# Down projection of the second chunk as seven f16 products, with its operand sums spread over ten pairs of units, and a fourth gate buffer for the other chunks

## The chip, the cores and the metric

The kernel runs on one core of a Trainium2 chip. A core has a matrix engine (TensorE, PE in the profile), a vector engine (VectorE, DVE), a scalar engine (ScalarE, ACT), a general engine (GpSimd, POOL) and a sync engine (SyncE, SP). Each runs its own queue of instructions in order; they wait for each other by semaphores. SP, ACT and POOL can issue transfers (DMAs) between main memory and the on-chip memories SBUF and PSUM. TensorE writes to PSUM, which has eight banks of 128 x 512 float32.

The metric is the device time of one execution in microseconds (us); lower is better. A time is given as the median of several executions.

## The reference

```
x  : 2048 x 448          wq : 448 x 4096      wo : 4096 x 448
k_cache, v_cache : 8 heads x 2048 x 256
w_gate, w_up : 448 x 1792                     w_down : 1792 x 448

xn = layernorm(x)
q  = xn @ wq                      16 heads of 256, two to each k/v head
k, v = the last 512 positions of the caches
o  = softmax(q k^T / 16) v
s  = o @ wo
g  = silu((gelu(xn @ w_gate) * (xn @ w_up)) @ w_down)
out = x + s * g
```

The change is in `g`: in the product with `w_down`, for 512 of the 2048 rows.

## The kernel before

The 2048 rows are 16 tiles of 128, and four chunks of 512 rows (`QC`, `NQC`). The kernel first computes `g` for all rows (the feed-forward stage), stores it to main memory (`g2d`, called g_all in the profile), then does the attention head by head, and at the end of each chunk the output projection with the rows' `g` (`burst`).

**Feed-forward.** The 1792 columns of w_gate and w_up are 14 blocks of 128 (`NF`). A unit is one block for one chunk: both products x w_gate and x w_up, into two banks. There are 56 units, numbered n, and the loop takes them in pairs (n, n+1); four are done ahead of it. The loop alternates between two sets of four banks, `cur` and `nxt`. The units of chunk 0 are 0 to 13, of chunk 1 14 to 27, of chunk 2 28 to 41, of chunk 3 42 to 55. After the matmuls of a pair (`gu_group`), ScalarE applies gelu to the gate bank (into `gl`, three buffers) and VectorE multiplies it with the up bank into `actT` (`gu_evac`, L522 and L523). `actT` holds two chunks, by chunk number modulo 2, in bf16. In the loop VectorE also does the layer norm of the later tiles (`ln_a`, `ln_b`, up to n = 28), ScalarE casts w_o to f16 (`cast_wt`, 16 casts), and VectorE forms sums of the cast parts (`sum_wt`, 16 sums). `CASTS` and `SUMS` are lists with the n from which each may be done; one or two are taken for each pair.

**Down projection.** `down(c, pairs)` multiplies the 512 rows of chunk c with w_down: for each of the four tiles 14 matmuls of 448 columns into a bank, then tanh on ScalarE (L533), then (tanh + 1) times the bank on VectorE into `g2w` (L534), then a store from SP into `g2d` (L537). `g2w` has three buffers (`NXR`), taken by the tile number modulo 3. `DOWN_AT` places it: chunk 0 after the pair n = 18, chunk 1 after n = 28. Chunks 2 and 3 follow within the first two steps of the attention loop (m = 0 and 1).

**Output projection.** `burst` already computes o @ wo by seven products instead of eight: both operands are cut in two halves in each direction, certain sums and differences of the quarters are formed beforehand by VectorE (`sums`, `sum_wt`), and seven products of quarters in f16, added up with signs, give the result.

**Queues and order.** The program order of each engine is the order in which the Python code calls `K.op`. `Plan` records what each operation reads and writes and makes it wait for the operations it depends on; `K.reuse` does that for memory that held something else. SP holds, in this order: the first loads, the transposes of the layer norm, the stores of the first two down projections, from n = 32 all loads of w_q, V and K (K is transposed on the way), then the transposes of the attention's probabilities (`dma_t` in `s_mm`) and the stores of the last two down projections. POOL holds the loads of w_o (`load_wt` at n = 14 and 30), then the loads of `g2` and x (`load_g2`, `xr`).

Of the kernel before, what the change touches and what calls it, by code (L numbers as in the profile page):

```python
# [5 lines left out]
ACT = mybir.ActivationFunctionType  # L6
ALU = mybir.AluOpType
BF16 = mybir.dt.bfloat16
F32 = mybir.dt.float32
F16 = mybir.dt.float16  # L10

LN_EPS = 1e-5
P = 128
# [155 lines left out]
def bass_recurrent_scan__sliding_block_cached__geglu_ffn__prompt_kernel(  # L169
# [12 lines left out]
    _, S, D = A_x.shape  # L182
    Hkv, Sk, Dh = A_k_cache.shape[1], A_k_cache.shape[2], A_k_cache.shape[3]
# [3 lines left out]
    F = B_w_gate.shape[1]  # L187
    NT = S // P
    QC = 512
    NQC = S // QC  # L190
    NF = F // P
    NJ = W // P
# [10 lines left out]
    NG = Hq // HG  # L203
    QS = 8
    Q0 = 4
    HC = QC // 2
    N2 = D // 2
    WS = 64.0

    es = ExitStack()  # L210
    with es:
        K = Plan(nc, es)
        base = [(nc.sbuf_base + 31) // 32 * 32]

        def place(name, shape, dt, at=None):
            size = {BF16: 2, F16: 2, F32: 4}[dt]
            for n in shape[1:]:
                size *= n
            size = (size + 31) // 32 * 32
            if at is None:  # L220
                at = base[0]
                base[0] += size
            assert at + size <= nc.sbuf_usable_end, (name, at + size, nc.sbuf_usable_end)
            return nc.alloc_sbuf_tensor_at(name, list(shape), dt, offset=at), at, at + size

        def sbuf_bufs(at, size, n):
            return [K.buf(at + i * size, size) for i in range(n)]
# [5 lines left out]
        ident, a_ident, _ = place("ident", [P, P], BF16)  # L233
        b_ident = K.buf(a_ident, 256)
        nhalf, a, _ = place("nhalf", [P, 1], F32)
        b_nhalf = K.buf(a, 4)
        epst, a, _ = place("epst", [P, 1], F32)
        b_epst = K.buf(a, 4)
        stats, a, _ = place("stats", [P, NT, 6], F32)
        b_stats = sbuf_bufs(a, 24, NT)  # L240
        mv, a, _ = place("mv", [P, NT, 2], F32)
        b_mv = sbuf_bufs(a, 8, NT)
        ve, a, _ = place("ve", [P, NT], F32)
        b_ve = sbuf_bufs(a, 4, NT)
        rstd, a, _ = place("rstd", [P, NT], F32)
        b_rstd = sbuf_bufs(a, 4, NT)
        NRS = 8
        rsum, a, _ = place("rsum", [P, NRS], F32)
        b_rsum = sbuf_bufs(a, 4, NRS)
        rden, a, _ = place("rden", [P, NRS], F32)  # L250
        b_rden = sbuf_bufs(a, 4, NRS)

        xnT, a, _ = place("xnT", [P, NK + 1, S], BF16)
        b_xnT = [[K.buf(), K.buf()] for t in range(NT)]
        NG2 = 2
        g2, a, _ = place("g2", [P, NG2, D], BF16)
        b_g2 = sbuf_bufs(a, D * 2, NG2)
        g2d = nc.dram_tensor("g2_all", [NT, P, D], BF16)
        b_g2d = [K.buf() for t in range(NT)]
        kT, a, _ = place("kT", [P, Hkv, 2, W], BF16)  # L260
        b_kT = sbuf_bufs(a, 2 * W * 2, Hkv)
        va, a, _ = place("va", [P, Hkv, NJ, Dh], BF16)
        b_va = [K.buf() for g in range(Hkv)]
        wq, a, _ = place("wq", [P, NK, HD], BF16)
        wqr, a, _ = place("wqr", [P, Hq, P], BF16)
        b_wql = [[K.buf() for i in range(3)] for g in range(NG)]
        NXR = 3
        xr, a, _ = place("xr", [P, NXR, D], BF16)
        b_xr = [[K.buf(a + (i * D + lo) * 2, (hi - lo) * 2) for lo, hi in ((0, CUT), (CUT, D))] for i in range(NXR)]
        g2w, _, _ = place("g2w", [P, NXR, D], BF16, at=a)  # L270
        b_g2w = sbuf_bufs(a, D * 2, NXR)
        tmp, a, _ = place("tmp", [P, 2, QC], F32)
        b_tmp = sbuf_bufs(a, QC * 4, 2)

        rw = base[0]
        NB = 4
        wt, _, rw_end = place("wt", [P, 7, Hq, N2], F16)
# [21 lines left out]
        b_wd = K.buf(a, at - a)  # L299
        actT, a, at = place("actT", [P, 2, NF, QC], BF16, at=at)  # L300
        b_actT = [sbuf_bufs(a + i * NF * QC * 2, QC * 2, NF) for i in range(2)]
        NGL = 3
        gl, a, at = place("gl", [P, NGL, QC], BF16, at=at)
        b_gl = sbuf_bufs(a, QC * 2, NGL)


        NPT, NPN, NP32 = 3, 3, 3
        pT, a, at = place("pT", [P, NPT, 2, 2, NJ, P], BF16, at=rf)
# [32 lines left out]
        def dma(q, o, i, reads=(), writes=()):  # L341
            K.op(q, lambda e, o=o, i=i: e.dma_start(o, i), reads, writes, dma=True)
# [4 lines left out]
        def act(o, i, func, reads, writes, scale=1.0):  # L347
            K.op("act", lambda e, o=o, i=i: e.activation(o, i, func, scale=scale), reads, writes)  # L348

        def add(eng, o, x, y, reads, writes, op=ALU.add):  # L350
            K.op(eng, lambda e: e.tensor_tensor(o, x, y, op), reads, writes)

        def mms(lst, reads, writes, after=()):
            def fn(e):
                ins = None
                for (o, l, r, st, sp) in lst:
                    ins = e.matmul(o, lhsT=l, rhs=r, start=st, stop=sp, skip_group_check=True)  # L357
                return ins
            return K.op("pe", fn, reads, writes, after=after)
# [159 lines left out]
        def gu_evac(n, b):  # L519
            c, f = divmod(n, NF)  # L520
            s = n % NGL
            act(gl[:, s, :], bank[b], ACT.Gelu_apprx_tanh, (b_ps[b],), (b_gl[s],))  # L522
            K.op("dve", lambda e: e.tensor_tensor(actT[:, c % 2, f, :], bank[b + 1], gl[:, s, :], ALU.mult),  # L523
                 (b_ps[b + 1], b_gl[s]), (b_actT[c % 2][f],))

        def down(c, pairs):
            for t4 in range(4):
                t = c * 4 + t4
                b = bk(pairs, t4)
                mms([(bank[b][:, 0:D], actT[:, c % 2, f, t4 * P:(t4 + 1) * P], wd[:, f, :], f == 0, f == NF - 1)  # L530
                     for f in range(NF)], [b_wd] + b_actT[c % 2], (b_ps[b],))
                s = t % 2
                act(tmp[:, s, 0:D], bank[b][:, 0:D], ACT.Tanh, (b_ps[b],), (b_tmp[s],), scale=0.5)  # L533
                K.op("dve", lambda e, t=t, b=b, s=s: e.scalar_tensor_tensor(  # L534
                    out=g2w[:, t % NXR, :], in0=tmp[:, s, 0:D], scalar=1.0, in1=bank[b][:, 0:D],
                    op0=ALU.add, op1=ALU.mult), (b_tmp[s], b_ps[b]), (b_g2w[t % NXR],))
                dma("sp", g2d[t], g2w[:, t % NXR, :], (b_g2w[t % NXR],), (b_g2d[t],))  # L537

        def ln_first(t):
            ln_stats(t)  # L540
# [58 lines left out]
        def load_k(g):  # L599
            dma_t(kT[:, g, :, :], A_k_cache[0, g, Sk - W:Sk, :], (), (b_kT[g],))  # L600

        def load_v(g):
            dma("sp", va[:, g, :, :],
                A_v_cache[0, g, Sk - W:Sk, :].rearrange("(j p) d -> p j d", p=P), (), (b_va[g],))

        def load_wq(g):
            lo, hi = g * HG * Dh, (g + 1) * HG * Dh
            dma("sp", wq[:, :, lo:hi], A_wq[0:K3, lo:hi].rearrange("(k p) f -> p k f", p=P), (), (b_wql[g][0],))
            for e in range(2):
                dma("sp", wqr[R * e:R * e + R, g * HG:(g + 1) * HG, :],  # L610
                    A_wq[K3:D, lo:hi].rearrange("p (h e f) -> p h e f", e=2, f=P)[:, :, e, :], (), (b_wql[g][1 + e],))
# [3 lines left out]
        def load_wt(j, e, n):  # L615
            dma("pool", wtb[:, WAT[j], :, :], wo_view[:, e, :, n * N2:(n + 1) * N2], (), b_wt[j])
# [5 lines left out]
        def sum_wt(o, x, y, i):  # L622
# [1 line left out]
            add("dve", wt[:, WAT[o], hs, :], wt[:, WAT[x], hs, :], wt[:, WAT[y], hs, :],  # L624
                [b_wt[x][i], b_wt[y][i]], b_wt[o][i:i + 1], ALU.subtract)

        CASTS = [(18, (j, i)) for j in (0, 4) for i in range(NB)] + [(40, (j, i)) for j in (2, 1) for i in range(NB)]
        SUMS = [(32, (4, 4, 0, i)) for i in range(NB)] + [
            (44, (o, x, y, i)) for i in range(NB) for o, x, y in ((5, 2, 4), (6, 5, 0), (3, 1, 5))]

        DOWN_AT = {NF + 5: 0, 2 * NF + 1: 1}
        gu_evac(0, 0)
        gu_evac(1, 2)
        gu_evac(2, 4)
# [3 lines left out]
        for n in range(4, NU, 2):  # L638
            gu_group((n, n + 1), cur)
            gu_evac(n, cur[0])  # L640
            ln_b()
            gu_evac(n + 1, cur[1])
            if ln_t[0] < 8 or n >= 12:
                ln_a()
            cur, nxt = nxt, cur
            if n == 4:
                load_x("sp", 12, 4)
            if n == 8:
                dma("sp", wd[:, :, :], B_w_down.rearrange("(f p) d -> p f d", p=P), (), (b_wd,))
            if n == 14:  # L650
                load_wt(0, 0, 0)
                load_wt(4, 0, 1)
            if n == 30:
                K.reuse([b for j in (1, 2, 3, 5, 6) for b in b_wt[j]])
                load_wt(2, 1, 1)
                load_wt(1, 1, 0)
            for i in range(2 if n >= 40 else 1):
                if CASTS and n >= CASTS[0][0]:
                    cast_wt(*CASTS.pop(0)[1])
            for i in range(2 if n >= 44 else 1):  # L660
                if SUMS and n >= SUMS[0][0]:
                    sum_wt(*SUMS.pop(0)[1])
            if n == 32:
                for g in range(NG):
                    load_wq(g)
                for g in range(Hkv):
                    load_v(g)
                for g in range(Hkv):
                    load_k(g)
            if n + 1 in DOWN_AT:  # L670
                down(DOWN_AT[n + 1], cur)
                cur, nxt = nxt, cur


        def q_group(n, pairs, more_act=False):
# [269 lines left out]
```

The softmax here doesn't subtract the row's maximum and nothing guards it: scores larger than these inputs give would overflow.

## Time and profile before

| | |
|---|---|
| median of nine runs | 548.33 us (547.67 to 549.05) |
| the profiled execution | 547.84 us, its span 546.1 us |
| granted TensorE clock | 1.00 |
| matmuls wd,actT (448 columns, bf16) | 224, 43.0 us busy |
| matmuls wt,sr and wt,oTh (224 columns, f16) | 512, 49.7 us busy, and 384, 38.3 us busy |
| cast of w_o, ScalarE, 128 x 896 | 16, mean 942 ns |
| sum of w_o parts, VectorE, 128 x 896 f16 | 16, mean 616 ns |
| sums in the burst, VectorE, 128 x 1024 f16 | 64, mean 683 to 692 ns |
| gate of a tile, VectorE (L534) | 16, mean 620 ns |
| tanh of a tile, ScalarE | mean 542 ns |
| gelu (128 x 512), product into actT | 597 ns and 688 ns |
| idle of VectorE before L534 for a store | 9.8 us in 2 waits |
| loads of w_q, V, K: first issue, landing | issued from 80.36 us; 9.2, 6.4 and 4.5 us (medians) |

The engines' rows give the busy time, its share of the span and the number of instructions. The matmul busy times are unions, so a group's busy time over its count is close to the pitch of its matmuls, while the mean of one contains the latency. In the timeline each row has the start, the duration, the engine, the line, the operation and the tiles; `x56` is the number of instructions merged in the row, and the bracket gives the idle time before it and what ended it. L357 is the helper `mms`, through which all matmuls but the transposes go, so matmuls are told apart by their tiles; L348 and L351 are the helpers `act` and `add`.

The feed-forward stage takes from about 12 us to 115 us of the span, the down projection of chunk 0 from 38 to 49 us, that of chunk 1 from 64 to 75 us. The attention loop begins at 115 us.

### The profile page before, as it was taken

The numbers are of one execution on the slowest core, as the hardware profiler recorded it, in microseconds if no ns is written. First come the engines' busy times: TensorE is split into PE (matmuls) and PEld (weight loads), VectorE is DVE, ScalarE is ACT, GpSimd is POOL, SyncE is SP. The second block draws the span as 40 slices with busy tenths as digits, with TensorE's granted clock in tenths as the row PEclk, the third lists the DMA queues.
The fourth block names the chain that finished last, engine by engine and source line by source line (L and its number), as shares of the span: only waits on it lengthen the run. The fifth ranks groups of instructions, "written<-read, shape, count | busy, mean of one in ns | idle before, by whom it ended". The sixth has DMA issues, their size and how long they took to land.

```text
span 546.1 us, 10453 instructions
## 1 busy us (share of the span) xinstructions
PE 537.1 (98%) x3955; PEld 294.3 (54%) x3980; DVE 349.6 (64%) x785; ACT 304.8 (56%) x770; POOL 38.8 (7%) x78
## 2 busy tenths in 40 slices
PE   8999989999999999999999999999999999999997
PEld 5554444445444444894444459644444884444487
DVE  6673726673356757943875777367668934876775
ACT  5433625854448858305875870388578206876820
POOL 1130400000010000003001000020000003001010
PEclk9999999999999999999999999999999999999999
DMA  9568279922264827401781680067556402863721
GB/s 292 124 189 127 60 174 315 205 58 71 75 104 95 149 66 136 97 2 48 166 152 46 150 151 10 17 139 145 104 87 153 79 2 68 164 154 82 151 53 34
DMA packets 171458, 61.34 MB, mean 112 GB/s; under 512 B 154960, under 2 KB 168272, under 8 KB 171408
## 3 DMA queue, kind: packets, MB, share of 16 engines
q1 hardware_dynamic: 167632, 51.39, 44.3%
q0 software_dynamic: 3008, 8.72, 6.7%
q8 instruction: 31, 0.51, 0.4%
q10 hardware_dynamic: 768, 0.57, 0.3%
q14 instruction: 19, 0.16, 0.1%
HBM read 19.76 MB, written 3.67 MB: 43 GB/s over the span
## 4 chain that ended last, share of the span: by engine, by line
PE 92%; DMA 3%; DVE 2%; ACT 2%; issue 1%; DVEq 0%; ACTq 0%
PE bank L357 92%; DMA g_all<-g2w 2%; ACT p L703 1%; DVE pn L710 1%; DMA x<-in_A_x_dram 0%; DVE rden L707 0%; DVE g2w L534 0%; DVE stats L404 0%; PE bank L455 0%; DVE qT L688 0%; ACT oTh L348 0%; DVE xn L430 0%; ACT xnT L348 0%; DVE mv L407 0%; PE bank L474 0%
## 5 line engine op out<-in xcount | busy, mean ns | idle before, releaser
L703 ACT ACTIVATE p<-bank 128x512 f32<-128x512 f32 x256 | 150.4, 596 | 24.8 <-DVE pn L710 19.6
L357 PE MATMUL bank<-pT,va 128*128 128x512 bf16 x512 | 120.8, 379 | 0.0
L357 PE MATMUL bank<-kT,qT 128*128 128x512 bf16 x487 | 117.8, 379 | 2.3 <-ACT qT L348 1.0
L710 DVE TENSOR_SCALAR pn<-p,rden 128x512 bf16<-128x512 f32 x256 | 113.0, 484 | 9.1 <-DMA pT<-pn 4.9
L357 PE MATMUL bank<-xnT,wq 64*128 64x512 bf16 x768 | 94.9, 376 | 0.0
L357 PE MATMUL bank<-xnT,wgu 64*128 64x512 bf16 (+2 forms) x768 | 84.0, 350 | 1.5 <-DVE g2w L534 1.4
L357 PEld LDWEIGHTS bank<-kT,qT 128*128 128x128 bf16 x512 | 49.4, 98 | 62.0 <-issue 3.8
L357 PEld LDWEIGHTS bank<-pT,va 128*128 128x128 bf16 x512 | 49.8, 98 | 60.6 <-DMA pT<-pn 1.9
L348 ACT ACTIVATE qT<-bank 128x512 bf16<-128x512 f32 x76 | 44.1, 596 | 55.4 <-PE bank L357 53.8
L688 DVE CAST qT<-bank 128x512 bf16<-128x512 f32 x52 | 35.1, 691 | 54.6 <-PE bank L357 54.6
L357 PEld LDWEIGHTS bank<-xnT,wq 64*128 64x128 bf16 x768 | 36.7, 94 | 46.3 <-ACT p L703 2.1
L357 PEld LDWEIGHTS bank<-xnT,wgu 64*128 64x128 bf16 x768 | 36.9, 94 | 38.5 <-DVE g2w L534 1.9
L348 ACT ACTIVATE gl<-bank 128x512 bf16<-128x512 f32 x56 | 33.2, 597 | 39.2 <-PE bank L357 36.0
L707 DVE RECIPROCAL rden<-rsum 128x2 f32<-128x2 f32 x128 | 21.1, 165 | 49.0 <-ACT p L703 49.0
L703 ACT ACTIVATION_READ_ACCUMULATOR p<-bank 128x1 f32 x256 | 51.7, 202 | 0.0
L523 DVE TENSOR_TENSOR actT<-bank,gl 128x512 bf16<-128x512 f32 x56 | 37.7, 688 | 21.5 <-PE bank L357 15.2
L357 PE MATMUL bank<-wt,sr 128*128 128x224 f16 x512 | 49.7, 259 | 0.0
L357 PEld LDWEIGHTS bank<-wt,sr 128*128 128x128 f16 x512 | 49.1, 98 | 0.0
L348 ACT ACTIVATE xnT<-bank 128x224 bf16<-128x224 f32 (+2 forms) x12 | 4.4, 398 | 71.5 <-PE bank L357 70.9
L357 PE MATMUL bank<-wd,actT 128*128 128x448 bf16 x224 | 43.0, 353 | 0.0
L728 DVE TENSOR_SCALAR oTh<-bank 128x512 f16<-128x512 f32 x62 | 42.3, 683 | 0.0
L348 ACT ACTIVATE oTh<-bank 128x512 f16<-128x512 f32 x66 | 38.9, 589 | 4.6 <-PE bank L357 4.6
(51 smaller groups left out, 351.4 us busy)
## 6 DMA issues: line engine op xcount, KB each, us to landing
wtb<-in_A_wo_dram POOLq DMA_DIRECT2D x4, 896.0 KB, 11.2
wq<-in_A_wq_dram SPq DMA_DIRECT2D x2, 1536.0 KB, 9.2
va<-in_A_v_cache_dram SPq DMA_DIRECT2D x8, 256.0 KB, 6.4
pT<-pn SPq DMA_TRANSPOSE x128, 2.8
g_all<-g2w SPq DMA_DIRECT2D x16, 112.0 KB, 2.1
xr<-in_A_x_dram POOLq DMA_DIRECT2D x15, 112.0 KB, 2.3
wd<-in_B_w_down_dram SPq DMA_DIRECT2D x1, 1568.0 KB, 7.6
g<-g_all POOLq DMA_DIRECT2D x14, 112.0 KB, 2.3
```

The lines of the kernel that those rows point to most:

```text
L348: K.op("act", lambda e, o=o, i=i: e.activation(o, i, func, scale=scale), reads, writes)
L357: ins = e.matmul(o, lhsT=l, rhs=r, start=st, stop=sp, skip_group_check=True)
L523: K.op("dve", lambda e: e.tensor_tensor(actT[:, c % 2, f, :], bank[b + 1], gl[:, s, :], ALU.mult), (b_ps[b + 1], b_gl[s]), (b_actT[c % 2][ ...
L688: K.op("dve", lambda v, s=s, b=b: v.tensor_copy(qT[:, s, 1, :], bank[b + 1]), (b_ps[b + 1],), (b_qT[s][1],))
L703: K.op("act", lambda e, b=b, r=r, z=z: e.activation(p32[:, z, :], bank[b], ACT.Exp, scale=att_scale, accum_out=rsum[:, r:r + 1]), (b_ps[b] ...
L707: K.op("dve", lambda e, r=r: e.reciprocal(rden[:, r - 1:r + 1], rsum[:, r - 1:r + 1]), b_rsum[r - 1:r + 1], b_rden[r - 1:r + 1])
L710: K.op("dve", lambda e, r=r - 1 + t, z=(n - 1 + t) % NP32, y=y, t=t: e.tensor_scalar(pn[:, y, t, :], p32[:, z, :], rden[:, r:r + 1], None, ...
L728: K.op("dve", lambda v, i=i, b=b: v.tensor_scalar(oTh[:, i, :], bank[b], WS, None, op0=ALU.mult), (b_ps[b],), (b_oT[i],))
```

## The change

1. **Seven products.** The down projection of chunk 1 goes from `down` to the new `down7`, and from behind n = 28 to behind n = 38. The 14 blocks of `actT` are cut in halves of 7 (`NH`), the 512 rows in halves of 256, the 448 columns of w_down in halves of 224. Four quarters of w_down are cast to f16 (`wdt`), three more are formed by `sum_wd`; four sums of act quarters by `sum_act` (`sd`). Seven products of 7 steps and 2 tiles each follow, 98 matmuls of 224 columns; VectorE adds the banks up (`plus`), ScalarE and VectorE form the gates (`gate`), into `g2x` with four buffers, and SP stores them. Chunk 1's act is written as f16 (`actTh`, in the place of `actT`).
2. **Spread.** `WD_CASTS` puts 8 casts on the pairs from n = 20 and `DN_SUMS` 12 sums on n = 26 to 38. The casts of w_o move from n = 18 and 40 to n = 34 and 46, its sums from n = 32 and 44 to n = 40 and 48 (three a pair from there), its second load from n = 30 to 36.
3. **Loads.** The temporary tiles lie where K, V and the first part of w_q will be. So the loads of w_q, V and K move from n = 32 to behind `down7`, in another order: half of w_q, two heads of K, the other half of w_q, V, the rest of K.
4. **Fourth buffer.** In `down` the gate buffer is taken by the tile's place in its chunk; the fourth is the first buffer of `g2`.

```diff
-        b_va = [K.buf() for g in range(Hkv)]
+        b_va = sbuf_bufs(a, NJ * Dh * 2, Hkv)
...
-        b_g2w = sbuf_bufs(a, D * 2, NXR)
+        g2w = [g2w[:, i, :] for i in range(NXR)] + [g2[:, 0, :]]
+        b_g2w = sbuf_bufs(a, D * 2, NXR) + b_g2[:1]
...
+        actTh, _, _ = place("actTh", [P, 2, NF, QC], F16, at=a)
...
+        wdt, b_wdt, a2 = temp("wdt", [P, 7, NH, N2], F16, b_kT[0].lo, 7)
+        sd, b_sd, a2 = temp("sd", [P, 4, NH, HC], F16, a2, 4)
+        cd, b_cd, a2 = temp("cd", [P, 3, D], F32, a2, 3)
+        th, b_th, a2 = temp("th", [P, 2, D], F32, a2, 2)
+        g2x, a, a2 = place("g2x", [P, 4, D], BF16, at=at)
+        b_g2x = sbuf_bufs(a, D * 2, 4)
...
-            K.op("dve", lambda e: e.tensor_tensor(actT[:, c % 2, f, :], bank[b + 1], gl[:, s, :], ALU.mult),
+            o = actTh if c == 1 else actT
+            K.op("dve", lambda e: e.tensor_tensor(o[:, c % 2, f, :], bank[b + 1], gl[:, s, :], ALU.mult),
...
-                    out=g2w[:, t % NXR, :], in0=tmp[:, s, 0:D], scalar=1.0, in1=bank[b][:, 0:D],
-                    op0=ALU.add, op1=ALU.mult), (b_tmp[s], b_ps[b]), (b_g2w[t % NXR],))
-                dma("sp", g2d[t], g2w[:, t % NXR, :], (b_g2w[t % NXR],), (b_g2d[t],))
+                    out=g2w[t4], in0=tmp[:, s, 0:D], scalar=1.0, in1=bank[b][:, 0:D],
+                    op0=ALU.add, op1=ALU.mult), (b_tmp[s], b_ps[b]), (b_g2w[t4],))
+                dma("sp", g2d[t], g2w[t4], (b_g2w[t4],), (b_g2d[t],))
+
+        def cast_wd(j, e, n, i):
+            fs = (slice(0, 4), slice(4, NH))[i]
+            fe = slice(e * NH + fs.start, e * NH + fs.stop)
+            act(wdt[:, j, fs, :], wd[:, fe, n * N2:(n + 1) * N2], ACT.Copy, (b_wd,), b_wdt[j:j + 1], scale=WS)
+
+        def sum_wd(o, x, y):
+            add("dve", wdt[:, o, :, :], wdt[:, x, :, :], wdt[:, y, :, :], [b_wdt[x], b_wdt[y]], b_wdt[o:o + 1], ALU.subtract)
+
+        def sum_act(c, k, i):
+            fs = (slice(0, 4), slice(4, NH))[i]
+            o = lambda e, r: (actTh[:, c, e * NH + fs.start:e * NH + fs.stop, r * HC:(r + 1) * HC],
+                              b_actT[c][e * NH + fs.start:e * NH + fs.stop])
+            S = lambda j: (sd[:, j, fs, :], b_sd[j:j + 1])
+            j, (x, bx), (y, by), op = ((3, o(0, 0), o(0, 1), ALU.subtract), (2, o(1, 1), S(3), ALU.subtract),
+                                       (0, S(2), o(0, 0), ALU.add), (1, o(1, 0), S(2), ALU.subtract))[k]
+            add("dve", S(j)[0], x, y, bx + by, S(j)[1], op)
+
+        def down7(c, one, other):
+            B1, B4, B6, B7, B5, B3 = one[0], one[0] + 1, one[1], one[1] + 1, other[0], other[0] + 1
...
+            def product(j, b, x, first=True):
+                lhs, bx = x
+                mms([(bank[b][:, t * N2:(t + 1) * N2], lhs(i)[:, t * P:(t + 1) * P], wdt[:, j, i, :],
+                      first and i == 0 and t == 0, False) for i in range(NH) for t in range(2)], bx + [b_wdt[j]], (b_ps[b],))
...
+            def gate(q, r, n):
+                act(th[:, q % 2, :], cd[:, q % 3, :], ACT.Tanh, b_cd[q % 3:q % 3 + 1], b_th[q % 2:q % 2 + 1], scale=0.5)
+                def end():
...
+                        out=g2x[:, 2 * r:2 * r + 2, n * N2:(n + 1) * N2], in0=two(th[:, q % 2, :]), scalar=1.0,
+                        in1=two(cd[:, q % 3, :]), op0=ALU.add, op1=ALU.mult),
...
+            product(0, B1, A(0, 0))
+            act(U2, bank[B1][:, 0:D], ACT.Copy, (b_ps[B1],), bU2, scale=F)
+            product(5, B6, S(2))
+            product(6, B7, S(3))
+            product(3, B4, A(1, 1))
+            product(4, B5, S(0))
+            product(2, B3, S(1))
+            product(1, B1, A(1, 0), False)
+            plus(U2, bU2, B6, U2, bU2)
+            plus(U3, bU3, B7, U2, bU2)
+            plus(cd[:, 0, :], b_cd[:1], B4, U3, bU3)
+            g0 = gate(0, 1, 0)
+            plus(cd[:, 1, :], b_cd[1:2], B5, U3, bU3)
+            g1 = gate(1, 1, 1)
+            plus(U2, bU2, B5, U2, bU2)
+            g0()
+            plus(cd[:, 2, :], b_cd[2:], B3, U2, bU2)
+            g1()
+            store(1)
+            g2_ = gate(2, 0, 1)
+            act(cd[:, 0, :], bank[B1][:, 0:D], ACT.Copy, (b_ps[B1],), b_cd[:1], scale=F)
+            g2_()
+            gate(3, 0, 0)()
+            store(0)
+            return (other[1], one[1]), (one[0], other[0])
...
-        CASTS = [(18, (j, i)) for j in (0, 4) for i in range(NB)] + [(40, (j, i)) for j in (2, 1) for i in range(NB)]
-        SUMS = [(32, (4, 4, 0, i)) for i in range(NB)] + [
-            (44, (o, x, y, i)) for i in range(NB) for o, x, y in ((5, 2, 4), (6, 5, 0), (3, 1, 5))]
-
-        DOWN_AT = {NF + 5: 0, 2 * NF + 1: 1}
+        CASTS = [(34, (j, i)) for j in (0, 4) for i in range(NB)] + [(46, (j, i)) for i in range(NB) for j in (2, 1)]
+        SUMS = [(40, (4, 4, 0, i)) for i in range(NB)] + [
+            (48, (o, x, y, i)) for i in range(NB) for o, x, y in ((5, 2, 4), (6, 5, 0), (3, 1, 5))]
+        WD_CASTS = [(20, (j, e, n, i)) for j, e, n in ((0, 0, 0), (4, 0, 1), (2, 1, 1), (1, 1, 0)) for i in range(2)]
+        DN_SUMS = [(26, sum_act, (1, k, 0)) for k in range(4)] + [(28, sum_act, (1, k, 1)) for k in range(4)] + [
+            (28, sum_wd, x) for x in ((4, 4, 0), (5, 2, 4), (6, 5, 0), (3, 1, 5))]
+
+        DOWN_AT = {NF + 5: 0, 39: 1}
...
-            if n == 30:
+            if n == 36:
                 K.reuse([b for j in (1, 2, 3, 5, 6) for b in b_wt[j]])
...
+            for i in range(1):
+                if WD_CASTS and n >= WD_CASTS[0][0]:
+                    cast_wd(*WD_CASTS.pop(0)[1])
+            for i in range(2 if n in (28, 30, 32, 34, 36) else 1):
+                if DN_SUMS and n >= DN_SUMS[0][0]:
+                    _, f, x = DN_SUMS.pop(0)
+                    f(*x)
...
-            for i in range(2 if n >= 44 else 1):
+            for i in range(3 if n >= 48 else 1):
...
-            if n == 32:
-                for g in range(NG):
-                    load_wq(g)
-                for g in range(Hkv):
-                    load_v(g)
-                for g in range(Hkv):
-                    load_k(g)
             if n + 1 in DOWN_AT:
...
+                if DOWN_AT[n + 1] == 1:
+                    cur, nxt = down7(1, cur, nxt)
+                else:
+                    down(DOWN_AT[n + 1], cur)
+                    cur, nxt = nxt, cur
+                if DOWN_AT[n + 1] == 1:
+                    K.reuse(b_kT + b_va)
...
+                    load_wq(0)
+                    for g in range(2):
+                        load_k(g)
+                    load_wq(1)
+                    for g in range(Hkv):
+                        load_v(g)
+                    for g in range(2, Hkv):
+                        load_k(g)
```

More of the change, by code (lines that the diff above doesn't have):

```diff
@@ L304, in bass_recurrent_scan__sliding_block_cached__geglu_ffn__prompt_kernel, with temp @@
         b_gl = sbuf_bufs(a, QC * 2, NGL)
+        NH = NF // 2
+        b_dn = []
+        def temp(name, shape, dt, at, n):
+            t, a, a2 = place(name, shape, dt, at=at)
+            b = sbuf_bufs(a, (a2 - a) // n, n)
+            b_dn.extend(b)
+            return t, b, a2
+        wdt, b_wdt, a2 = temp("wdt", [P, 7, NH, N2], F16, b_kT[0].lo, 7)
[4 more added lines that the diff above has]
+        b_g2x = sbuf_bufs(a, D * 2, 4)
         NPT, NPN, NP32 = 3, 3, 3
@@ L533, in down @@
                 act(tmp[:, s, 0:D], bank[b][:, 0:D], ACT.Tanh, (b_ps[b],), (b_tmp[s],), scale=0.5)
-                K.op("dve", lambda e, t=t, b=b, s=s: e.scalar_tensor_tensor(
-                    out=g2w[:, t % NXR, :], in0=tmp[:, s, 0:D], scalar=1.0, in1=bank[b][:, 0:D],
-                    op0=ALU.add, op1=ALU.mult), (b_tmp[s], b_ps[b]), (b_g2w[t % NXR],))
-                dma("sp", g2d[t], g2w[:, t % NXR, :], (b_g2w[t % NXR],), (b_g2d[t],))
+                K.op("dve", lambda e, t4=t4, b=b, s=s: e.scalar_tensor_tensor(
+                    out=g2w[t4], in0=tmp[:, s, 0:D], scalar=1.0, in1=bank[b][:, 0:D],
+                    op0=ALU.add, op1=ALU.mult), (b_tmp[s], b_ps[b]), (b_g2w[t4],))
@@ new lines, in down7, with plus, store @@
+        def down7(c, one, other):
+            B1, B4, B6, B7, B5, B3 = one[0], one[0] + 1, one[1], one[1] + 1, other[0], other[0] + 1
+            F = 1.0 / WS
+            A = lambda e, r: (lambda i: actTh[:, c, e * NH + i, r * HC:(r + 1) * HC], b_actT[c][e * NH:(e + 1) * NH])
+            S = lambda i: (lambda k: sd[:, i, k, :], b_sd[i:i + 1])
+            U2, U3 = tmp[:, 0, 0:D], tmp[:, 1, 0:D]
+            bU2, bU3 = b_tmp[:1], b_tmp[1:]
+            def product(j, b, x, first=True):
+                lhs, bx = x
+                mms([(bank[b][:, t * N2:(t + 1) * N2], lhs(i)[:, t * P:(t + 1) * P], wdt[:, j, i, :],
+                      first and i == 0 and t == 0, False) for i in range(NH) for t in range(2)], bx + [b_wdt[j]], (b_ps[b],))
+            def plus(o, bo, b, V, bV):
+                K.op("dve", lambda e: e.scalar_tensor_tensor(
+                    out=o, in0=bank[b][:, 0:D], scalar=F, in1=V, op0=ALU.mult, op1=ALU.add), [b_ps[b]] + bV, bo)
+            def gate(q, r, n):
+                two = lambda x: x.rearrange("p (t d) -> p t d", t=2)
+                act(th[:, q % 2, :], cd[:, q % 3, :], ACT.Tanh, b_cd[q % 3:q % 3 + 1], b_th[q % 2:q % 2 + 1], scale=0.5)
+                def end():
+                    K.op("dve", lambda e: e.scalar_tensor_tensor(
+                        out=g2x[:, 2 * r:2 * r + 2, n * N2:(n + 1) * N2], in0=two(th[:, q % 2, :]), scalar=1.0,
+                        in1=two(cd[:, q % 3, :]), op0=ALU.add, op1=ALU.mult),
+                        (b_th[q % 2], b_cd[q % 3]), b_g2x[2 * r:2 * r + 2])
+                return end
+            def store(r):
+                for t in range(2 * r, 2 * r + 2):
+                    dma("sp", g2d[c * 4 + t], g2x[:, t, :], (b_g2x[t],), (b_g2d[c * 4 + t],))
+            product(0, B1, A(0, 0))
[23 more added lines that the diff above has]
+            return (other[1], one[1]), (one[0], other[0])
@@ L659, in bass_recurrent_scan__sliding_block_cached__geglu_ffn__prompt_kernel @@
                     cast_wt(*CASTS.pop(0)[1])
-            for i in range(2 if n >= 44 else 1):
+            for i in range(3 if n >= 48 else 1):
                 if SUMS and n >= SUMS[0][0]:
                     sum_wt(*SUMS.pop(0)[1])
-            if n == 32:
-                for g in range(NG):
-                    load_wq(g)
-                for g in range(Hkv):
-                    load_v(g)
-                for g in range(Hkv):
-                    load_k(g)
-            if n + 1 in DOWN_AT:
-                down(DOWN_AT[n + 1], cur)
-                cur, nxt = nxt, cur
+            if n + 1 in DOWN_AT:
+                assert not DN_SUMS or DN_SUMS[0][0] > n, DN_SUMS
+                if DOWN_AT[n + 1] == 1:
[5 more added lines that the diff above has]
+                    K.reuse(b_kT + b_va)
+                    for b in [y for x in b_wql for y in x]:
+                        b.old.extend(y for x in b_dn for y in x.readers + [x.writer] if y is not None)
+                    load_wq(0)
[6 more added lines that the diff above has]
+                        load_k(g)
         def q_group(n, pairs, more_act=False):
```

## The prediction

> **What bounds the kernel now.** I read the busy times of the page first, then the chain that ended last, then the timeline of the feed-forward stage where the change sits. The profiled execution took 547.84 us, its span is 546.1 us (1.74 us lie around it); the median of nine runs is 548.33. I sum against the span and subtract the result from the median.
>
> ```profile
> PE 537.1 (98%) x3955; PEld 294.3 (54%) x3980; DVE 349.6 (64%) x785; ACT 304.8 (56%) x770; POOL 38.8 (7%) x78
> ...
> PE 92%; DMA 3%; DVE 2%; ACT 2%; issue 1%; DVEq 0%; ACTq 0%
> ```
>
> TensorE is busy for 98% of the span, so whatever shortens its stream, or an idle hole in it, moves the end. The chain in order of time shows one place in the feed-forward stage where TensorE doesn't lead:
>
> ```profile
> 66.70 0.66 issue
> 67.36 0.63 DVE g2w L534
> 67.99 0.02 issue
> 68.01 11.22 DMA g_all<-g2w
> 79.23 0.03 issue
> ...
> 79.35 0.63 DVE g2w L534
> 79.98 0.05 issue
> 80.03 40.98 PE bank L357 x378
> ```
>
> The 11.22 us are no loss of that size: TensorE had other work meanwhile. The timeline of the stretch shows the loss:
>
> ```profile
> 63.87 10.77 PE L357 MATMUL bank<-wd,actT 128*128 128x448 bf16 x56
> ...
> 74.57 0.82 PE L357 MATMUL bank<-xnT,wgu 64*128 64x512 bf16 x6
> ...
> 79.35 0.62 DVE L534 SCALAR_TENSOR_TENSOR g2w<-tmp,bank 128x448 bf16<-128x448 f32 x1 [6.01 <-DMA g_all<-g2w]
> ...
> 80.03 0.60 PE L357 MATMUL bank<-xnT,wgu 64*128 64x512 bf16 x4 [1.40 <-DVE g2w L534]
> ```
>
> This is the second chunk's down projection. Its fourth gate needs the buffer whose store was issued at 68.01 and landed 11.2 us later (the median store lands in 2.1). VectorE stands for 6.01 us, the fourth tile's bank isn't freed, and the next pair but one (n=32) stops after its first eight matmuls. From 74.57 to 115.43, where the query projection begins, lie 13 pairs of units. A pair without a wait takes 3.022 us (the next twelve follow one another at that pitch), 13 x 3.022 = 39.29, and 40.86 passed: **the hole is 1.57 us** (1.40 recorded idle, plus the tail of the modelled end of the matmul before it).
>
> **The products.** Removed: 56 matmuls of 448 columns, 63.87 to 74.57 = 10.70 us (191 ns each). Added: 7 products x 7 steps x 2 tiles = 98 matmuls of 224 columns in f16. The output projection runs just this form:
>
> ```profile
> 223.06 6.30 PE L357 MATMUL bank<-wt,oTh 128*128 128x224 f16 x64
> 229.20 12.43 PE L357 MATMUL bank<-wt,sr 128*128 128x224 f16 x128
> 241.46 3.23 PE L357 MATMUL bank<-wt,oTh 128*128 128x224 f16 x32
> 244.62 0.82 PE L357 MATMUL bank<-xnT,wq 64*128 64x512 bf16 x6
> ```
>
> 224 matmuls in 244.62 - 223.06 = 21.56 us: 96.25 ns each, with no gap between products. 98 x 0.09625 = 9.43 us, so **-1.27**. Bounds: the middle line alone (229.20 to 241.46, 95.8 ns) gives 9.39; 99.7 ns, the busy time of the wt,oTh group over its count (38.3/384), gives 9.77. I take 96.25, a whole burst with its seams.
>
> [...]
>
> **The hole.** The second chunk's gates now go into g2x, four buffers of their own, so no gate waits for a store: **-1.57** (at least the 1.40 recorded). The fourth buffer of the plain blocks I cost at nothing: the first chunk's fourth gate waited 3.82 us for a store, yet TensorE ran on, and the last two blocks' gates waited only for ScalarE and TensorE. Its price is that the first g2 load waits for the store of tile 15 (issued at 147.8). POOL, which issued that load at 67.0, queues behind it only loads of g2 and xr; the xr loads stood until about 150 before as well, and g2 isn't read before the first burst at 223.
>
> **ScalarE's casts.** Eight casts of w_down, one a pair from n=20, take the slots that eight casts of w_o leave; those go to n=34 and later, the other eight to n=46. A cast of 128x896 takes 0.942, the 672-wide ones lie between 0.597 (128x512) and that. A pair with two casts fills ScalarE: two gelus and two casts took 2.98 of 3.02 us from 95.0 to 104.9 before, four pairs in a row, and TensorE never waited. The new order has such pairs at n=40, 42 and four in a row from 46. Cost 0; without cover at most the excess of the means, 2 x 0.597 + 2 x 0.942 - 3.02 = 0.06 a pair, 0.4 over six.
>
> **VectorE's sums.** Eight sums of act: 128x1024 took 0.687, 768 wide less (0.55 on the slope of 896 to 1024). Four of w_down, 1568 wide: 0.98 on that slope, between 0.687 and 1.08 (0.616 in proportion). VectorE has 2.5 us of work in a pair with layer norm, 1.3 without. At n=26 and 28 it comes to some 3.2 and 3.7 against 3.02, about 0.8 late, gone by n=32. A pair's second unit was evacuated at 65.85 and its bank wanted 1.9 us later (63.87 + 3.02 + 0.86), so that stays hidden. At n=36 two sums of w_down make 3.2. By my clock the products start at 63.87 + 5 x 3.022 = 78.98; sums 5 and 6 end at 78.4 and 79.4 and are wanted at 80.3 and 81.7; the last, queued behind the evacuation of n=38, ends at 81.6 and is wanted at 83.0. Three sums of w_o a pair from n=48 make 1.26 + 1.8 = 3.06 a pair: a few tenths late in all, inside the same 1.9. Cost 0, up to 1.3 if a product does wait.
>
> **The seam after the products.** Pair n=40 takes a bank evacuated at about 81 and the banks of the second and third product, which VectorE adds up by 83.7, long before 88.4. Pair n=42 needs the rest at 91.4: the last copy of the first bank ends near 89.2 (ScalarE, 0.54), the tanh near 89.8, the last gate (0.62) near 90.5. Cost 0, or up to 0.16 at each of two seams, the idle seen where TensorE passes from projection to scores (165.49).
>
> **The moved loads.** All loads of w_q, V and K now stand on SP behind the products' stores: issue from 80.36 to about 90.9. In their old place they kept the DMA engines full until about 114 (33.5 us). What comes first is half of w_q, wanted at 112.6, and K of two heads, at 118.6. The w_q loads landed in 7.8 to 10.6 us, the K transposes in 3.3 to 7.0, so I have w_q by 102 and K by 107. The rest lands by 125; behind it on SP stand the first transposes of probabilities (ready near 121.8), read after 143. Cost 0.
>
> **Sum:** -1.27 - 1.57 = -2.84; span 543.3, median 548.33 - 2.84 = **545.5**.
>
> **The rivals.** (B) The hole goes, but TensorE waits inside the products: the thinnest cover is the 1.4 us of the last w_down sum. If VectorE runs 2.7 late there (1.4 + 1.27), the products' gain is gone: 546.8. For it: 12 sums by n=38 on an engine also evacuating; against: the slack worked out above. (C) **Slower:** the late loads. If half of w_q must share the engines with all that is queued behind it, it lands with the last byte, 90.9 + 33.5 = 124.4; the query projection then starts 11.8 late, which makes 557.3. It decides against the change once w_q lands after about 116.5 (112.6 + 2.84 + 1.1). For it: the DMA engines were full in that stretch, and one store there took 11.2; against: no w_q load took more than 10.6, and it now stands first. (D) Full pairs: ScalarE and VectorE both at 3.0 or more from n=46 to 54; if each of the six pairs gave back 0.3, 1.8 is lost: 547.3, no change. Against: four such pairs on ScalarE before without a wait. (E) The change doesn't do what it says: a wait of the old size appears elsewhere, only the products count: 548.33 - 1.27 = 547.1.
>
> **How the numbers follow.** A 0.69, B 0.10, E 0.04, D 0.07, C 0.10. A measurement tells about 0.2%, 1.1 us, from no change; A, B and (just) E are faster than 547.2: 0.83; D is the same: 0.07; C slower: 0.10. A's own range: products 9.39 to 9.77 (-1.31 to -0.93), hole 1.40 to 1.57, seams 0 to 0.32: 545.4 to 546.3, and some 0.3 for the medians, 545.1 to 546.6. The range reaches on to B and E: 544.9 to 547.2.
>
> **What would show it.** Matmuls of wdt in f16, 98 of them, in some 9.4 us from about 79.0; no wait of VectorE on a g_all store; no idle TensorE between 64 and 112.6; query projection from 112.6. A wait of TensorE named VectorE sd or wdt is B, one on w_q or kT is C, rising idle after n=46 is D.

## The result, and the profile after

| | before | changed |
|---|---|---|
| median | 548.23 us (29 runs) | **545.56 us** (9 runs, 545.11 to 546.85) |
| ratio, 95% interval | | 0.9956 [0.9948, 0.9965] |
| profiled execution, span | 547.84, 546.1 | 546.65, 544.8 |
| first matmul of the query projection | 115.43 | 113.07 |

The forecast was 545.5, with a range of 544.9 to 547.2. On another chip the same two kernels gave 546.07 (11 runs) and 548.08: 0.9962 [0.9949, 0.9975].

In the changed kernel the helper through which the matmuls go is line 374, and the product into act is line 541. First the page's busy times and its chain by engine:

```profile
PE 536.4 (98%) x3997; PEld 297.9 (55%) x4022; DVE 361.4 (66%) x803; ACT 311.9 (57%) x780; POOL 39.3 (7%) x78
...
PE 92%; DMA 3%; DVE 2%; ACT 2%; issue 1%; ACTq 0%; DVEq 0%
```

VectorE and ScalarE have 12 and 7 us more to do, TensorE 0.7 less busy time. The shares of the chain are the same, so they say nothing of the change; its pieces in order of time (start, length, what) do:

```profile
10.29 108.36 PE bank L374 x1008
118.67 0.70 DVE qT L802
119.43 12.27 PE bank L374 x63
```

One unbroken piece of TensorE reaches from 10.29 to 118.65, where before it was cut at 66.70 and taken up again at 80.03. The hole is gone. The timeline of TensorE shows the block itself:

```profile
79.39 1.52 PE L374 MATMUL bank<-wdt,actTh 128*128 128x224 f16 x14
80.74 2.85 PE L374 MATMUL bank<-wdt,sd 128*128 128x224 f16 x28
83.42 1.50 PE L374 MATMUL bank<-wdt,actTh 128*128 128x224 f16 x14
84.76 2.85 PE L374 MATMUL bank<-wdt,sd 128*128 128x224 f16 x28
87.45 1.50 PE L374 MATMUL bank<-wdt,actTh 128*128 128x224 f16 x14
88.88 0.82 PE L374 MATMUL bank<-xnT,wgu 64*128 64x512 bf16 x6
```

98 matmuls from 79.39 to 88.88, 9.49 us, with no bracket of a wait at any of the seams.

The two profiled spans differ by 1.3 only. The changed kernel's profiled execution was one of its slower ones, and lost 1.1 us in the attention, some 375 us behind the products. The timeline there:

```profile
465.84 0.88 DVE L824 TENSOR_SCALAR pn<-p,rden 128x512 bf16<-128x512 f32 x2 [1.50 <-DMA pT<-pn]
...
466.95 1.90 PE L374 MATMUL bank<-pT,va 128*128 128x512 bf16 x8 [0.88 <-DMA pT<-pn]
```

A transpose of probabilities landed after 5.0 us where the median takes 2.7. The profile of the second measurement has no such row, and a span of 543.6. To keep this scatter out, the experiments are also read by a stretch inside the feed-forward stage: from the first matmul of chunk 0's down projection to the first of the query projection. These two rows, before and in the changed kernel, are in the timeline:

```profile
37.95 10.77 PE L357 MATMUL bank<-wd,actT 128*128 128x448 bf16 x56
...
115.43 0.81 PE L357 MATMUL bank<-xnT,wq 64*128 64x512 bf16 x6
```

```profile
38.36 10.77 PE L374 MATMUL bank<-wd,actT 128*128 128x448 bf16 x56
...
113.07 0.81 PE L374 MATMUL bank<-xnT,wq 64*128 64x512 bf16 x6
```

The stretch was 115.43 - 37.95 = **77.48 us** before and 113.07 - 38.36 = **74.71** in the changed kernel (74.70 in the second measurement): **-2.77**.

### The profile page after: what moved, and what is told of

It reads as the page before. It is cut to its first block, busy times and chain, and to the rows that moved or that the text cites. A ratio compares the mean times of both kernels' runs of the same rounds, so it can differ in the third digit from the quotient of the medians.

```text
span 544.8 us, 10579 instructions
## 1 busy us (share of the span) xinstructions
PE 536.4 (98%) x3997; PEld 297.9 (55%) x4022; DVE 361.4 (66%) x803; ACT 311.9 (57%) x780; POOL 39.3 (7%) x78
## 4 chain that ended last, share of the span: by engine, by line
PE 92%; DMA 3%; DVE 2%; ACT 2%; issue 1%; ACTq 0%; DVEq 0%
PE bank L374 92%; DMA pT<-pn 2%; ACT p L817 1%; DVE pn L824 1%; DMA x<-in_A_x_dram 1%; ACTq L359 0%; DVE rden L821 0%; ACT qT L365 0%; DVE qT L802 0%; DVE oTh L842 0%; DVE stats L421 0%; DVE xn L447 0%; ACT oTh L365 0%; PE bank L472 0%; ACT xnT L365 0%
## 5 line engine op out<-in xcount | busy, mean ns | idle before, releaser
L374 PE MATMUL bank<-wt,oTh 128*128 128x224 f16 x384 | 38.3, 259 | 0.3 <-ACT oTh L365 0.3
L374 PEld LDWEIGHTS bank<-wt,oTh 128*128 128x128 f16 x384 | 36.7, 98 | 1.8 <-ACT oTh L365 1.1
```

## The experiments

| kernel | stretch | median | ratio to the kernel before, run beside it |
|---|---|---|---|
| before | 77.48 | 548.0 to 548.2 | |
| fourth buffer alone | 75.90 | 546.50 | 0.9973 [0.9962, 0.9983] |
| before, second w_o load later | 76.25 | 546.57 | 0.9974 [0.9966, 0.9983] |
| plain block late | 75.91, 75.91 | 546.52, 546.78 | 0.9978 [0.9968, 0.9988], 0.9977 [0.9967, 0.9987] |
| plain block late, three buffers | 75.98 | 546.88 | 0.9977 [0.9967, 0.9987] |
| changed | 74.71, 74.70 | 545.56, 546.07 | 0.9956 [0.9948, 0.9965], 0.9962 [0.9949, 0.9975] |
| changed, three buffers | 74.93, 74.70 | 546.08, 546.77 | 0.9976 [0.9963, 0.9989], 0.9971 [0.9958, 0.9985] |
| changed, loads in old order | 74.70, 74.70 | 546.18, 545.61 | 0.9968 [0.9954, 0.9982], 0.9963 [0.9951, 0.9975] |
| changed, sums bunched | 79.54 | 550.67 | 1.0051 [1.0032, 1.0071] |
| changed, loads tied late | 78.36 | 550.99 | 1.0056 [1.0044, 1.0068] |

### Where the hole came from

**The fourth buffer alone**, in the kernel before.

```diff
-        b_g2w = sbuf_bufs(a, D * 2, NXR)
+        g2w = [g2w[:, i, :] for i in range(NXR)] + [g2[:, 0, :]]
+        b_g2w = sbuf_bufs(a, D * 2, NXR) + b_g2[:1]
...
-                    out=g2w[:, t % NXR, :], in0=tmp[:, s, 0:D], scalar=1.0, in1=bank[b][:, 0:D],
+                    out=g2w[t4], in0=tmp[:, s, 0:D], scalar=1.0, in1=bank[b][:, 0:D],
...
```

> The kernel before with the fourth gate buffer alone. Theory (the gain is the removed hole, 1.57, plus the products, 1.2): the second chunk's fourth gate no longer waits for the store that lands late, the hole goes, -1.57: about 546.7, query projection at 113.9 instead of 115.4. Rival (the gain is all in the products and their placing, the hole is filled by other work anyway): no change, 548.2.

The stretch shrank by 1.58. VectorE's fourth gate and TensorE's pair n = 32 in the timeline:

```profile
75.33 0.62 DVE L535 SCALAR_TENSOR_TENSOR g<-tmp,bank 128x448 bf16<-128x448 f32 x1 [2.03 <-ACT tmp L349]
```

```profile
78.42 0.81 PE L358 MATMUL bank<-xnT,wgu 64*128 64x512 bf16 x6
```

The gate runs at 75.33, behind its tanh, where it ran at 79.35; the matmuls that began at 80.03 after a wait begin at 78.42 without one. The theory holds: more than half of the gain (1.58 of 2.77) needs no products.

**The second load of w_o held back**, in the kernel before, with its three buffers.

```diff
-            if n == 30:
+            if n == 32:
                 K.reuse([b for j in (1, 2, 3, 5, 6) for b in b_wt[j]])
+                for b in b_wt[2] + b_wt[1]:
+                    b.old.append(b_actT[0][2].writer)
```

> The kernel before, with three buffers and the block in its old place, but the second load of w_o held back until the product of unit 30 into act is done (about 78 us instead of 64.5). Theory: without that load the stores of the second chunk land in about 2 us and the hole goes: about 546.7. Rival (the store is late for another reason, the layer norm's transposes ahead of it on SP): hole and 548.2 as before.

The timeline, first POOL's load, then VectorE's fourth gate:

```profile
79.70 2.38 POOL L342 DMA_DIRECT2D wtb<-in_A_wo_dram  x2 [13.89 <-DVE actT L523]
```

```profile
76.22 0.62 DVE L534 SCALAR_TENSOR_TENSOR g2w<-tmp,bank 128x448 bf16<-128x448 f32 x1 [2.02 <-ACT tmp L348]
```

With the load 15 us later, the gate waits for its tanh only, though the buffers are three. The store that took 11.2 us lands in 1.6. POOL's two loads of g, which stand behind the load of w_o, moved with it (from 67.00 to 82.07); but with the fourth buffer alone they go out only at 148.36, and there the same store still took 10.8. So the store was late because it met the load of w_o. In its second chunk this kernel has no hole; the 0.35 that its stretch is longer than that of the fourth buffer alone lies ahead of it: from block to block pass 26.26 us, where 25.91 passed there (chunk 0's gate is read below).

**The plain block behind n = 38**, with four buffers and with three: no products, but place, loads and w_o casts as in the changed kernel.

```diff
-            o = actTh if c == 1 else actT
+            o = actT
...
+        WD_CASTS, DN_SUMS = [], []
         DOWN_AT = {NF + 5: 0, 39: 1}
...
-                if DOWN_AT[n + 1] == 1:
-                    cur, nxt = down7(1, cur, nxt)
-                else:
-                    down(DOWN_AT[n + 1], cur)
-                    cur, nxt = nxt, cur
+                down(DOWN_AT[n + 1], cur)
+                cur, nxt = nxt, cur
```

With three buffers, besides:

```diff
-                    out=g2w[t4], in0=tmp[:, s, 0:D], scalar=1.0, in1=bank[b][:, 0:D],
+                    out=g2w[t % NXR], in0=tmp[:, s, 0:D], scalar=1.0, in1=bank[b][:, 0:D],
...
```

> The changed kernel with the second chunk's down projection as 56 plain bf16 matmuls at its new place behind n = 38, four buffers, loads and w_o casts as changed; casts and sums for the products left out. Theory: hole gone, products not there: 1.2 above the changed kernel, about 546.8; its block takes 10.7 us. Rival (moving the block, loads and casts costs or gains something by itself): another time than that of the fourth buffer alone by over 0.5.

> As the plain block behind n = 38, but with the three gate buffers by tile number of the kernel before. Theory (the hole came from a store that landed in 11.2 us because it met the second load of w_o and not from three buffers as such): behind n = 38 no other transfer runs, the store lands in about 2 us, no hole: about 546.8, equal to the one with four buffers. Rival (three buffers make the hole wherever the block stands): the hole is back, about 548.3.

75.91 and 75.98: neither has the hole, and with four buffers the stretch equals that of the fourth buffer alone to 0.01. The second load of w_o still goes out where it did (at 64.60 and 65.29; 64.53 before), though the code now has it at n = 36; it's the block that has moved away from it, and with three buffers all four stores of the block land in 1.6 to 1.7 us. So, within the stretch, the new place, the moved loads and the moved casts cost nothing and gain nothing beyond the hole. There are three ways to be rid of it: another buffer, another place, or a later load.

### What the products gain

Plain block late against the changed kernel is the products with their casts and sums: 75.91 - 74.70 = **1.21**. The plain block and the row behind it, in the timeline:

```profile
79.05 10.77 PE L374 MATMUL bank<-wd,actT 128*128 128x448 bf16 x56
89.74 0.82 PE L374 MATMUL bank<-xnT,wgu 64*128 64x512 bf16 x6
```

It takes 89.74 - 79.05 = 10.69, where the products take 9.49. Both kernels were run again on one chip:

> The changed kernel again, beside three of its variants on one chip. Theory: 2.8 below the kernel before of the same call.

> The plain block behind n = 38 again, beside the changed kernel. Theory: 1.2 above the changed kernel in the same call, all of it the products.

The stretches repeat to 0.01. The medians, 546.07 and 546.78, are 0.7 apart and the ratios differ by 0.0015 (0.8 us) with overlapping intervals, so the full time alone wouldn't have shown the 1.21. The kernels with products scatter more (544.84 to 547.46, against 546.19 to 547.92 of the plain block, whose lowest run is 1.35 above).

### The cover of the sums

Cover is the time by which a piece of work ends before it is wanted.

**The 12 sums bunched** on three pairs.

```diff
-        DN_SUMS = [(26, sum_act, (1, k, 0)) for k in range(4)] + [(28, sum_act, (1, k, 1)) for k in range(4)] + [
-            (28, sum_wd, x) for x in ((4, 4, 0), (5, 2, 4), (6, 5, 0), (3, 1, 5))]
+        DN_SUMS = [(34, sum_act, (1, k, 0)) for k in range(4)] + [(34, sum_act, (1, k, 1)) for k in range(4)] + [
+            (34, sum_wd, x) for x in ((4, 4, 0), (5, 2, 4), (6, 5, 0), (3, 1, 5))]
...
-            for i in range(2 if n in (28, 30, 32, 34, 36) else 1):
+            for i in range(4):
```

> The changed kernel with the 12 sums for the products bunched on the pairs n = 34, 36 and 38, four each. Theory (the spread hides them): VectorE reaches the last four, of 0.97 us, at about 82.6 us of the span; the second product, wanted at 80.7, waits for the second of them, until about 84.5: 3 to 4 us lost, about 549. Rival (the slack is wide, the spread isn't needed): as the changed kernel, 545.6.

VectorE and TensorE in the timeline, and the granted clock in windows of half a microsecond, for the line of the matmuls (the columns: window, its length, busy time and number of matmuls and of weight loads, clock, DMA share, GB/s):

```profile
81.41 3.87 DVE L368 TENSOR_TENSOR wdt<-wdt 128x1568 f16<-128x1568 f16 x4
```

```profile
78.81 1.51 PE L374 MATMUL bank<-wdt,actTh 128*128 128x224 f16 x14
83.44 4.41 PE L374 MATMUL bank<-wdt,sd 128*128 128x224 f16 x28 [3.12 <-DVE wdt L368]
87.69 1.50 PE L374 MATMUL bank<-wdt,actTh 128*128 128x224 f16 x14
```

```profile
83.00:83.50 0.50, 0.06 (x1) 0.06 (x2) 0.75 0.00 0
...
84.50:85.00 0.50, 0.50 (x5) 0.40 (x4) 0.50 0.00 0
...
86.50:87.00 0.50, 0.50 (x6) 0.47 (x5) 0.83 0.00 0
87.00:87.50 0.50, 0.50 (x8) 0.50 (x7) 1.00 0.00 0
```

The second product waited until 83.44 for the second of the four late sums, as the theory says; TensorE stood idle for 3.12 us. But the two products behind it took 4.41 instead of 2.85: the clock stood at half until about 86.7. In all the stretch grew by 4.84, of which a third is no waiting. The spread is needed.

### The cover of the moved loads

**Loads tied late**: the w_q loads, and so all that stands behind them on SP, held back until unit 50's product into act.

```diff
-                    load_wq(0)
...
+            if n == 50:
+                for x in b_wql:
+                    for b in x:
+                        b.old.append(b_actT[1][n - 42].writer)
+                load_wq(0)
...
```

> The changed kernel with the loads of w_q, V and K held back on SP until the product of unit 50 into act (about 108 us of the span instead of 91.8), to find the end of their cover. Theory (w_q lands 7.6 to 10.6 us after issue and had some 10 us to spare): w_q and its remainder land at 117 to 119, the query projection starts 4 to 6 us late: 549.5 to 551.5, and TensorE waits for the w_q loads. Rival (it needs all that is queued behind): 20 us or more late.

SP's first load of w_q, then TensorE at the start of the query projection, in the timeline:

```profile
107.51 0.38 SPq L359 DMA_DIRECT2D wq<-in_A_wq_dram  x1
```

```profile
116.17 0.82 PE L374 MATMUL bank<-xnT,wq 64*128 64x512 bf16 x6 [3.49 <-DMA wqr<-in_A_wq_dram]
...
117.03 1.25 PE L374 MATMUL bank<-xnT,wq 64*128 64x512 bf16 x6
...
118.47 3.23 PE L374 MATMUL bank<-xnT,wq 64*128 64x512 bf16 x18
```

The first w_q load was issued at 107.51, 19.18 us behind the end of the products at 88.33; in the changed kernel it was 2.88 us (91.76 - 88.88), so it went out 16.30 later. The projection began at 116.17 instead of 88.33 + 24.19 = 112.52 (end of the products plus eight pairs), 3.65 late. So the loads had 16.30 - 3.65 = **12.65 us to spare**, and need not wait for what is queued behind them: rival C's mechanism is denied. Here too the matmuls that follow are slow (the clock in windows, columns as above):

```profile
116.50:117.00 0.50, 0.50 (x8) 0.23 (x5) 1.00 1.20 275
117.00:117.50 0.50, 0.50 (x6) 0.24 (x4) 0.80 1.39 209
117.50:118.00 0.50, 0.50 (x4) 0.18 (x2) 0.50 0.49 49
...
120.50:121.00 0.50, 0.50 (x6) 0.29 (x4) 0.78 0.98 385
```

From 116.17 to the last twelve at 122.61 pass 6.44 us, against 4.74 in the changed kernel (113.07 to 117.81). 3.65 + 1.70 = 5.35 is what the median shows (550.99 - 545.56 = 5.4).

**Loads in the old order** behind the products (w_q, V, K), run on two chips.

```diff
-                    load_wq(0)
-                    for g in range(2):
-                        load_k(g)
-                    load_wq(1)
+                    for g in range(NG):
+                        load_wq(g)
                     for g in range(Hkv):
                         load_v(g)
-                    for g in range(2, Hkv):
+                    for g in range(Hkv):
                         load_k(g)
```

> The changed kernel with the loads behind the products in the old order: w_q, V, then K. Theory: K of the first head is issued at about 108 and landed by 113, wanted at 119: no change, 545.6; the new order is spare cover. Rival (the order is what saves the move): K late, 547 or more.

> The changed kernel with the loads in the old order again. Theory (the order is spare cover): within 0.3 of the changed kernel in the same call. Rival (it earns 0.5): 0.5 or more above.

The stretch is 74.70 both times; the medians lie above the changed kernel once (by 0.6, not run beside it) and below it once (by 0.5, run beside it). No effect is seen; the new order is spare cover.

### The fourth buffer of the plain blocks

**The changed kernel with three buffers** (the edit shown above), on two chips.

> The changed kernel with three gate buffers by tile number for the plain blocks. Theory (once the second chunk has buffers of its own, the fourth plain buffer is worth nothing): as the changed kernel, about 545.6; the first chunk's fourth gate waits about 3.8 us again without stopping TensorE. Rival (the fourth buffer earns part of the gain): 0.5 or more above.

> The changed kernel with three gate buffers again. Theory (the fourth plain buffer is worth nothing): within 0.3 of the changed kernel in the same call. Rival (it earns 0.5, as the medians of two different calls would have it): 0.5 or more above.

Inconclusive in the medians: 0.5 and 0.7 above the changed kernel, with overlapping intervals (0.9971 [0.9958, 0.9985] against 0.9962 [0.9949, 0.9975], run side by side). The stretch says 0.23 in one execution and 0.00 in the other. In the first, VectorE and then TensorE after chunk 0:

```profile
51.93 0.62 DVE L552 SCALAR_TENSOR_TENSOR g2w<-tmp,bank 128x448 bf16<-128x448 f32 x1 [4.65 <-DMA g_all<-g2w]
```

```profile
52.18 0.38 PE L374 MATMUL bank<-xnT,wgur 64*128 64x512 bf16 x2
52.61 0.82 PE L374 MATMUL bank<-xnT,wgu 64*128 64x512 bf16 x6
```

The second row should have begun at 52.40, 0.22 after the first. What decides is how long after the end of chunk 0's block its fourth gate starts. In the five executions with three plain buffers it started 2.74, 2.75, 3.28, 3.43 and 3.55 us after it, and TensorE lost 0, 0, 0.07, 0.22 and 0.35 ahead of the second chunk's block: the cover ends at 3.21, and from there each tenth is lost in full. With four buffers the loss was never over 0.01. That is what the buffer is seen to earn; the rest of the 0.5 to 0.7 stays open.

## Why the prediction was right

**Products, -1.27.** The term measured 1.21: the block took 9.49 for 9.43 forecast, against 10.70. The price from the output projection's burst (96.25 ns a matmul) was 0.6 ns low.

**Hole, -1.57.** The fourth buffer alone gave 1.58. The step that tied it to a late store was right; that the store was late because of the w_o load was not said. Holding the load back shows it, and the block in another place agrees.

**Fourth buffer at nothing.** Right for the profile before, mis-sized by up to 0.35 in others. In the profile before, the gate started 51.40 - 48.65 = 2.75 us after the block, 0.46 inside its cover, and when the store lands varies by more than that. The step "yet TensorE ran on" read one execution and didn't ask how near the edge it was; the cover could have been worked out as for the other pairs (3.02 + 0.86 until the bank is wanted, less the gate's 0.62, makes 3.26).

**Casts and sums at nothing.** The two sizes taken from a slope measured 968 ns (0.98 forecast) and about 0.55. The profiled execution runs 0.41 late from its start; on its own clock the last w_down sum ended at 81.89 against a forecast of 81.6 + 0.41, and was wanted at 83.42. Full pairs from n = 46 (rival D) cost nothing: eight pairs took 24.19 for 24.18.

**Seams and loads at nothing.** The last gate ended at 90.89 (90.5 + 0.41 forecast). Spare time of w_q: 12.65 measured, 10.6 forecast (112.6 - 102).

**Sum.** 2.84 forecast, 2.77 in the stretch, 2.67 between the medians. That the median itself came within 0.1 of the forecast is partly luck: the second measurement gave 546.07. The ratios, 0.9956 and 0.9962, make 2.4 and 2.1 of 548.2. The mean ratio of all six measurements of kernels with products and their sums and loads on time is 0.9966, that of the five measurements of plain blocks without the hole 0.9976: of the 1.21 only some 0.5 us is seen in the full time, where a single ratio is known to about 0.6 us. So part may be given back in the attention, as the profiled execution did with its 1.1 us. Two of the six profiles of these kernels with products lost 0.8 or more on TensorE waiting for a transpose of probabilities, none of the six with plain blocks. Whether that is chance or the shifted time against the transfers wasn't tried and stays open.

**Rivals.** The mechanism of B (a late sum stops the products) is real, as the bunched sums show, but its price was too low: I priced a wait by its length, and in both runs with some 3 us or more of idle time TensorE paid half as much again in clock. The same is missing from C's 557.3.

## What to carry to other kernels

Before trading arithmetic, look in the timeline for a hole next to the code in question: here one more buffer was worth more than seven products for eight (1.58 us against 1.21), and holding back a load as much (1.23). A product replaced by smaller ones is priced well from a place in the same kernel that already runs that form, seams included (9.43 us forecast, 9.49 measured), and only if the sums it needs are spread so that they end before they are wanted (bunched, they lengthened the stretch by 4.84 us). Where an effect is below the scatter of the full time, measure a stretch between two matmuls that bracket it.

## What the runs showed of the hardware

**The clock after a hole.** A hole of 1.40 us (before) left the granted clock at 1.00 in every window from 76 to 86 us. After 3.12 us (bunched sums) and 3.49 (loads late) it fell to 0.50, in the first case at 83.2 us of the span, just before TensorE resumed, in the second at 117.3, 1.1 us after it had. It stayed there for 3.4 us each time (until 86.7 and 120.7; these times are worked out from the windows above, 0.75 and 0.80 where it fell, 0.83 and 0.78 where it came back), and cost 1.6 and 1.7 us on top of the wait. This price doesn't look fixed. 3.4 us at half clock lower the mean clock of an execution by 0.003; of the eleven executions of these two kernels seven have a mean of 0.996 or 0.997 and three one of 0.994, about twice that time by this estimate (551.29, 551.73 and 551.98 us). One, of the bunched sums, has 0.999, as all other kernels have at least, and at 548.79 it is the fastest of the eleven, 3.2 above the changed kernel's median, which fits the wait alone. What makes the clock fall, and how long an idle stretch it takes, isn't shown.

**A small store beside a large load.** A store of 112 KB that lands in 2.1 us in the median took 11.2 when 1.8 MB of w_o were loaded from POOL's queue meanwhile, and with that load moved away it landed in 1.6 and its gate no longer waited.
